# Block attention with a top-1 expert layer: one written order of four rounds for TensorE, VectorE and ScalarE

## The chip, the core and the metric

The kernel runs on one core of one Trainium2 chip. TensorE multiplies matrices (PE in the profile, and PEld for its weight loads), VectorE (DVE), ScalarE (ACT) and GpSimd (POOL) do the elementwise work, SyncE (SP) issues the transfers. The metric is the device time of one execution in microseconds, smaller is better.

## The reference

```python
def _attn_ref(q, k, v) -> np.ndarray:
...
    scores = scale * np.matmul(q, k.transpose(0, 1, 3, 2))
...
    mask = block_i >= block_j
    scores = np.where(mask, scores, -1000000000.0)
    scores = scores - np.max(scores, axis=-1, keepdims=True)
    attn = np.exp(scores)
    attn = attn / (np.sum(attn, axis=-1, keepdims=True) + 1e-09)
    return np.matmul(attn, v).astype(np.float32)

def _moe_ref(x, w_gate, w_output_gate, w1, w2) -> np.ndarray:
...
    logits = x @ w_gate
    e_idx = np.argmax(logits, axis=1)
...
    for e in range(E):
        mask = e_idx == e
...
        h = np.maximum(x[mask] @ w1[e], 0.0)
        ye = h @ w2[e]
        out[mask] = gate_w[mask, None] * eom[mask, e, None] * ye
    return out.astype(np.float32)
```

Attention over 8 batches of 8 heads, 576 positions of 64 elements each, with a mask by blocks of 64 positions, comes first; its output is the input of a layer in which each token goes to one of eight experts.

## The kernel before, in words

The work of the attention is cut into 32 pairs of heads (`Pair`, numbered p), four pairs to a batch. A pair goes through these steps, each in a round of its own, and four rounds g carry one pair further; in every round several pairs are at work, at different steps:

- `fetch` loads q and k (`nat`, six transfers on SP); `split` casts them to 16 bits on ACT (`sp0`, two pairs of buffers) and takes the remainder on POOL (`sp1`); `turn` moves both through a transposing transfer into `tr` (four buffers).
- `max_tile` 0, 1 and 2 multiply q by k into score tiles of PSUM, from which DVE takes the negated maxima of the five row tiles (`nmx`, `nmz`); `turn_max` transposes them on PE and ACT copies them out (`qe`).
- `prob_tile` 0 to 3 multiply again, with the maxima and the mask as further products, and ACT takes the exponential (`pc13`, `pc0`, `pc2`, `pcr`). Its 16-bit remainder (`lpc`, `lpcr`) is made by DVE and POOL.
- `values_odd` and `values` 0 and 1 multiply the probabilities by v (`vn`, and its 16-bit halves `vh` from ACT and `vl` from POOL) into the one tile of `ps_v`; DVE divides by the sums (`xn`), SP stores it to `x_d`, and `turn_x` transposes it on PE for the routing, copied out by ACT (`xT`).
- After the fourth pair of a batch `finish_batch` computes the routing: logits, their maxima, ranks and weights, in small operations on PE, DVE and ACT.

All score tiles, transposes and logits take the three two-bank PSUM tiles of the pool `ps_s` in rotation (`banks()`): a tile can be written when the reader of the third tile before it is done. Before the change PE's instructions stand in program order (`manual_schedule`); a list scheduler orders those of the other engines, and `high_priority` marks the maxima. The first expert's weights are loaded and split from round 120 on; from about 600 us the kernel runs the experts alone, with code that the change leaves alone.

Of the kernel before, what the change touches and what calls it, by code (L numbers as in the profile page):

```python
# [10 lines left out]
F32 = mybir.dt.float32  # L11
# [9 lines left out]
P = 128  # L21
# [5 lines left out]
def block_attention_top1_moe(  # L27
# [18 lines left out]
    R0 = 64  # L46
# [45 lines left out]
    class Pair:  # L92
# [55 lines left out]
        def max_tile(self, i):  # L148
            if i == 0:
                self.nmx = small.tile([P, NT, 2], F32, name="nmx")  # L150

            def products(os, n, c0):
                m = P * (n + 1)
                main = [o[:, c0:c0 + m].rearrange("p (n x) -> p n x", x=P) for o in os]
                for ab in range(2):
                    nc.tensor.matmul(main[ab], self.asks(0, ab, n, n + 1)[:, 0], self.keys(0, ab, 0, n + 1), start=True, stop=False)  # L156
                for ab in range(2):
                    half = slice(64 * ab, 64 * ab + 64)
                    nc.tensor.matmul(
                        main[ab][:, n, 64:P], mq[half], mk[half], start=False, stop=True  # L160
                    )
                for ab in range(2):
                    nc.tensor.matmul(
                        os[ab][:, c0 + m:c0 + m + R0], self.asks(0, ab, n, n + 1)[:, 0], self.odd(0, ab, 0, R0), start=True, stop=True
                    )

            if i < 2:
                ps = banks()
                os = [ps[:, ab] for ab in range(2)]
                if i == 0:  # L170
                    products(os, 2, 0)
                    for ab in range(2):
                        nc.tensor.matmul(os[ab][:, 448:512], self.odd(0, ab, 0, P), self.odd(0, ab, 0, R0), start=True, stop=True)  # L173
                    parts = ((2, 0, 448), (4, 448, 512))
                else:
                    products(os, 1, 0)
                    products(os, 0, 320)
                    parts = ((1, 0, 320), (0, 320, 512))
                for t, c0, c1 in parts:
                    with tc.high_priority(offset=60):  # L180
                        last_max[0] = nc.vector.tensor_reduce(self.nmx[:, t, :], ps[:, :, c0:c1], AX.X, ALU.max, negate=True)  # L181
            else:
                os = [banks().rearrange("p a n -> p (a n)") for ab in range(2)]
                products(os, 3, 0)
                self.nmz = nmzs[self.p % 2]
                for ab in range(2):
                    with tc.high_priority(offset=60):
                        last_max[0] = nc.vector.tensor_reduce(self.nmx[:, 3, ab:ab + 1], os[ab][:, 0:S], AX.X, ALU.max, negate=True)  # L188
                with tc.high_priority(offset=60):
                    nc.vector.tensor_scalar(  # L190
                        self.nmz.rearrange("p t (h c) -> p t h c", h=2)[:, :, :, 0], self.nmx, 1.0 / MS, None, ALU.mult
                    )
# [8 lines left out]
        def prob_tile(self, i):  # L201
# [4 lines left out]
            ps = banks()  # L206
# [37 lines left out]
            if i != 1:  # L244
                for ab in (slice(0, 1), slice(1, 2)) if i == 0 and self.p < NPR - 4 else (slice(0, 2),):
                    eng = nc.gpsimd if ab.stop == 1 else nc.vector
                    eng.tensor_tensor(self.pl[i][:, ab], self.pt[i][:, ab], self.high(i)[:, ab], ALU.subtract)  # L247
# [25 lines left out]
        def values(self, ab):  # L273
# [13 lines left out]
            if ab == 0:  # L287
                return
# [7 lines left out]
            )  # L296
            to = x_d[self.b * S:(self.b + 1) * S, self.hp * P:(self.hp + 1) * P]
# [697 lines left out]
    def round_of(g):  # L995

        r = g % 4
        for fn in events.get(g, ()):
            fn()
# [6 lines left out]
        if r == 0:  # L1006
            do(0, "max_tile", 0)
            do(8, "prob_tile", 3)
            do(12, "values", 1)
        elif r == 1:  # L1010
            do(1, "max_tile", 1)
            do(5, "prob_tile", 0)
        elif r == 2:
# [12 lines left out]
    with tc.manual_schedule(engines={mybir.EngineType.PE}):  # L1026
# [119 lines left out]
```

## Time and profile before

| | |
|---|---|
| median of 3 runs | 981.88 us (981.39 to 984.54) |
| the profiled execution | 982.18 us |
| its span, first to last instruction | 980.2 us |
| PE busy | 820.9 us (84%) |
| DVE busy | 567.9 us (58%) |
| ACT busy | 456.7 us (47%) |
| POOL busy | 349.9 us (36%) |
| granted TensorE clock, mean | 0.857 |

The shares are means over the whole span, in which the attention (to about 570 us) and the experts (from about 600 us) behave differently. The granted clock is a share of 2.4 GHz; at any one time it is at 1.00 or at 0.50 (1.2 GHz), and values between are means over time. In the profile L181 and L188 are the maxima, L117 the casts of q and k, L243 the exponentials, L156 the score products, L213 the products of the probability tiles, L284 the first product of the values, L306 the output transposes, L197 and L199 the transposed maxima and their copy.

### The profile page before, as it was taken

How to read it: one execution, taken by the hardware profiler on the slowest of the kernel's cores; microseconds unless marked ns; L12 is line 12 of the kernel's file. 1: busy time of each engine (PE TensorE's matmuls, PEld its weight loads, DVE VectorE, ACT ScalarE, POOL GpSimd, SP SyncE). 2: the span in 40 equal slices, each digit the busy share in tenths (PEclk: the TensorE clock that was granted, in tenths of full speed). 3: DMA queues.
4: the chain of work that ended last, by engine and by line, in shares of the span. 5: the costliest groups of instructions: out<-in, count | busy, mean ns of one | idle time of the engine just before them, and what ended most of it. 6: DMA issues, size and time to landing. Idle time of an engine off the chain costs nothing. (4 is left out here: it accounts for less than half of the span.)

```text
span 980.2 us, 22497 instructions
## 1 busy us (share of the span) xinstructions
PE 820.9 (84%) x8893; PEld 586.8 (60%) x8912; DVE 567.9 (58%) x922; ACT 456.7 (47%) x700; POOL 349.9 (36%) x389
## 2 busy tenths in 40 slices
PE   2787868777878868778786899899999999999995
PEld 1464646555556646555564686667766777677762
DVE  7835544544544544656556335778685868686560
ACT  2644433324333333344334421767675767585650
POOL 5644344234243243342505534633223234241101
PEclk9986876776776777879687789999999999999998
DMA  6766684464454474545336205697999997972331
GB/s 158 153 146 143 134 132 87 93 94 97 102 115 85 96 113 97 104 93 97 51 74 187 66 26 195 172 311 210 294 325 327 298 303 231 299 220 66 131 108 35
DMA packets 277154, 148.72 MB, mean 152 GB/s; under 512 B 230864, under 2 KB 249328, under 8 KB 277040
## 3 DMA queue, kind: packets, MB, share of 16 engines
q1 hardware_dynamic: 268992, 127.90, 52.4%
q0 software_dynamic: 8048, 19.29, 6.2%
q8 instruction: 72, 1.18, 0.5%
q14 instruction: 42, 0.34, 0.1%
HBM read 126.03 MB, written 19.34 MB: 148 GB/s over the span
## 5 line engine op out<-in xcount | busy, mean ns | idle before, releaser
L872 PEld LDWEIGHTS <-w1b 128*128 128x128 f16 (+1 forms) x2208 | 177.1, 98 | 26.2 <-issue 4.8
L872 PE MATMUL ps_s<-xt,w1b 128*128 128x256 f16 (+5 forms) x1920 | 175.1, 253 | 0.4 <-DVE w1b L751 0.3
L901 PE MATMUL ps_o<-w2b,hh 128*128 128x512 f16 (+1 forms) x541 | 162.9, 380 | 0.8 <-ACT hh L880 0.5
L751 DVE TENSOR_TENSOR w2b<-w2f,w2b 128x1024 bf16<-128x1024 f32 x80 | 92.7, 1220 | 90.1 <-ACT w2b L749 83.7
L181 DVE TENSOR_REDUCE nmx<-ps_s 128x2 f32<-128x896 f32 (+3 forms) x128 | 82.1, 683 | 82.6 <-PE ps_s L173 76.1
L156 PE MATMUL ps_s<-tr 64*128 64x384 f16 (+3 forms) x256 | 53.1, 346 | 78.7 <-ACT pc L243 47.5
L284 PE MATMUL ps_v<-vn,pc 128*128 128x65 f32 x512 | 116.8, 348 | 0.0
L146 POOL TENSOR_TENSOR vl<-vn,vh 128x448 f16<-128x448 f32 x32 | 33.2, 1037 | 226.0 <-ACT vh L145 174.8
L118 POOL TENSOR_TENSOR sp<-nat,sp 128x256 f16<-128x256 f32 (+1 forms) x126 | 100.2, 815 | 30.2 <-ACT sp L117 26.2
L247 DVE TENSOR_TENSOR lpc<-pc 128x512 f16<-128x512 f32 (+1 forms) x64 | 53.5, 836 | 98.9 <-ACT pc L243 98.8
L901 PE MATMUL ps_o<-w2b,hl 128*128 128x512 f16 x280 | 106.4, 380 | 1.2 <-DVE hl L881 0.2
L910 POOL DMA_INDIRECT out_dram<-ys,ids x38 | 50.0, 1317 | 155.2 <-ACT ys L909 91.0
L213 PE MATMUL ps_s<-tr,tr 64*128 64x384 f16 (+5 forms) x768 | 98.5, 340 | 0.0
L284 PEld LDWEIGHTS ps_v<-vn,pc 128*128 128x128 f32 x512 | 94.9, 246 | 4.3
L243 ACT ACTIVATE pc<-ps_s 128x1024 f32<-128x1024 f32 (+1 forms) x96 | 83.5, 878 | 24.7 <-PE ps_s L213 14.9
L751 DVE TENSOR_TENSOR w1b<-w1f,w1b 128x1024 bf16<-128x1024 f32 x80 | 93.0, 1219 | 1.8 <-ACT w1b L749 1.5
L213 PEld LDWEIGHTS <-tr 64*128 64x128 f16 (+1 forms) x1152 | 53.1, 110 | 67.6 <-issue 40.1
L901 PEld LDWEIGHTS <-hh 128*128 128x128 f16 x560 | 54.4, 98 | 62.6 <-issue 0.8
L117 ACT CAST sp<-nat 128x256 f16<-128x256 f32 (+1 forms) x124 | 47.5, 427 | 92.5 <-DMA tr<-sp 67.0
L213 PE MATMUL ps_s<-tr 64*128 64x256 f16 (+5 forms) x384 | 66.4, 341 | 26.6 <-DVE nmx L188 14.4
L749 ACT CAST w1b<-w1f 128x1024 f16<-128x1024 f32 x80 | 78.5, 1046 | 4.3 <-DMA w1f<-in_moe_w_dram 4.1
L749 ACT CAST w2b<-w2f 128x1024 f16<-128x1024 f32 x80 | 77.6, 1043 | 1.3 <-DMA w2f<-in_moe_w_dram 1.3
(210 smaller groups left out, 1573.3 us busy)
## 6 DMA issues: line engine op xcount, KB each, us to landing
w1f<-in_moe_w_dram SPq DMA_DIRECT2D x80, 512.0 KB
w2f<-in_moe_w_dram SPq DMA_DIRECT2D x80, 512.0 KB
nat<-in_k_dram SPq DMA_DIRECT2D x64, 128.0 KB
nat<-in_q_dram SPq DMA_DIRECT2D x64, 128.0 KB
vn<-in_v_dram SPq DMA_DIRECT2D x64, 128.0 KB
x_d<-xn SPq DMA_DIRECT2D x32, 256.0 KB
hh<-in_moe_w_dram SPq DMA_DIRECT2D x4, 512.0 KB
hl<-in_moe_w_dram SPq DMA_DIRECT2D x4, 512.0 KB
```

The costliest lines, as they stand in the source:

```text
L118: last_lo[0] = lo.tensor_tensor(sl[:, h], nat, sh[:, h], ALU.subtract)
L156: nc.tensor.matmul(main[ab], self.asks(0, ab, n, n + 1)[:, 0], self.keys(0, ab, 0, n + 1), start=True, stop=False)
L181: last_max[0] = nc.vector.tensor_reduce(self.nmx[:, t, :], ps[:, :, c0:c1], AX.X, ALU.max, negate=True)
L213: nc.tensor.matmul(os[ab], ks(kc, ab), qs(qc, ab), start=j == 0, stop=j == 3)
L243: last_exp[0] = nc.scalar.activation(self.pt[i], ap, AF.Exp, scale=SCALE)
L247: eng.tensor_tensor(self.pl[i][:, ab], self.pt[i][:, ab], self.high(i)[:, ab], ALU.subtract)
L284: nc.tensor.matmul(o, part(self.pt[1]), self.vn[:, ab], start=False, stop=False)
L749: nc.scalar.copy(hi, src)
L751: eng.tensor_tensor(lo[at], src[at], hi[at], ALU.subtract)
L872: nc.tensor.matmul(ph[:, f4].rearrange("p (h n) -> p h n", n=w), wv[:, cc, f, :], xv[:, cc], start=(k == 0), stop=(k == 3 * KD - 1))
L901: nc.tensor.matmul(py, hv[:, f, h], wv[:, f, :], start=(k == 0), stop=(k == 3 * KF - 1))
L910: nc.gpsimd.indirect_dma_start(out=out, out_offset=IOA(ap=ids[i][0:w, h, 0:1].bitcast(U32), axis=0), in_=ys[0:w], in_offset=None, bounds_c ...
```

## The change

PE, DVE and ACT now all run in program order, and the rounds are written anew. The maxima's transposes move from the end of a round to the start of the next, the values of both halves one round ahead; normalising and storing become steps of their own; the remainders (`lows`) are placed apart from the exponentials. The loads, casts and transposed loads of a pair, which stood at the head of a round, stand at its end, with new round numbers. The last row tile's maxima took two score tiles, one for each head of the pair, 576 columns each; now both heads' 512 main columns share one tile, and the 64 odd columns of each are written into a free corner (columns 256 to 320) of the tile of `prob_tile` 2, which uses 256 columns a bank (`max_rest`).

```diff
-            at(base - 12, lambda p=p: make(p))
-            at(base - 9, lambda p=p: pairs[p].split(0, nc.scalar.copy, nc.gpsimd))
-            at(base - 8, lambda p=p: pairs[p].split(1, nc.scalar.copy, nc.gpsimd))
-        at(base - 7, lambda p=p: pairs[p].turn(0))
-        at(base - 6, lambda p=p: pairs[p].turn(1))
+            at(base - 14, lambda p=p: make(p))
+            at(base - 11 if p > 3 else 2 * p - 3, lambda p=p: pairs[p].split(0, nc.scalar.copy, nc.gpsimd))
+            at(base - 10 if p > 3 else 2 * p - 2, lambda p=p: pairs[p].split(1, nc.scalar.copy, nc.gpsimd))
+        at(base - 7 if p > 3 or p == 1 else 2 * p - 1, lambda p=p: pairs[p].turn(0))
+        at(base - 6 if p > 3 or p == 1 else 2 * p, lambda p=p: pairs[p].turn(1))
     for p in range(NPR):
-        at(4 * p + 5, lambda p=p: pairs[p].fetch_v())
-        at(4 * p + 8, lambda p=p: pairs[p].split_v())
+        at(4 * p + 4, lambda p=p: pairs[p].fetch_v())
+        at(4 * p + 7, lambda p=p: pairs[p].split_v())
+        at(4 * p + 13, lambda p=p: pairs[p].store())
...
         if r == 0:
+            do(4, "turn_max")
+            do(12, "norm")
             do(0, "max_tile", 0)
             do(8, "prob_tile", 3)
-            do(12, "values", 1)
         elif r == 1:
             do(1, "max_tile", 1)
             do(5, "prob_tile", 0)
+            do(9, "lows", 3)
...
         elif r == 2:
             do(6, "prob_tile", 1)
+            do(6, "lows", 0)
             do(2, "max_tile", 2)
-            do(14, "turn_x")
+            do(10, "values_odd")
+            do(10, "values", 0)
         else:
-            do(7, "prob_tile", 2)
-            do(11, "values_odd")
-            do(11, "values", 0)
-            do(3, "turn_max")
+            ps = banks() if g < 4 * NPR + 4 else None
+            do(7, "prob_tile", 2, ps)
+            do(3, "max_rest", ps)
+            do(7, "lows", 2)
+            do(11, "values", 1)
+            if g < 4 * NPR + 11:
+                do(15, "turn_x")
+        for fn in events.get(g, ()):
+            fn()
         pay_later()
 
-    NG = 4 * NPR + 11
+    NG = 4 * NPR + 10
...
-    with tc.manual_schedule(engines={mybir.EngineType.PE}):
+    with tc.manual_schedule(engines={AT.PE, AT.Activation, AT.DVE}):
...
+        def max_rest(self, ps):
+            self.odds([ps[:, ab] for ab in range(2)], 3, 256)
+            self.nmz = nmzs[self.p % 2]
+            nmr = small.tile([P, 2], F32, name="nmr")
+            last_max[0] = nc.vector.tensor_reduce(nmr, ps[:, :, 256:320], AX.X, ALU.max, negate=True)
+            nc.vector.tensor_tensor(self.nmx[:, 3, :], self.nmx[:, 3, :], nmr, ALU.min)
+            nc.vector.tensor_scalar(
+                self.nmz.rearrange("p t (h c) -> p t h c", h=2)[:, :, :, 0], self.nmx, 1.0 / MS, None, ALU.mult
+            )
```

Three places show what moves. The first is ACT around the first exponential of pair 15; before the change it reads so (`pcr` is the fourth exponential of pair 14, `sp` the casts of q and k of pair 20, `vh` that of v of pair 15, `pc` the first two exponentials of pair 15):

```order
L243 ACTIVATE pcr<-ps_s 128x576 [waits PE_49,Activation_49]
L117 CAST sp_4095<-nat 128x5x64 [waits DMAHW7_49,DMAHW6_49,Pool_49]
L117 CAST sp_4095<-nat 128x5x64 [waits DMAHW5_49]
L117 CAST sp_4095<-nat 128x4x64
L145 CAST vh_101<-vn_99 128x7x64 [waits DMAHW6_49,DMAHW0_49,PE_49]
L243 ACTIVATE pc_3941<-ps_s 128x1024 [waits PE_49]
L117 CAST sp_4095<-nat 128x4x64
L243 ACTIVATE pc_3942<-ps_s 128x1024 [waits PE_49,Activation_49]
```

With the change, the same casts of pair 20 (here `sp_4071`) stand behind the exponentials of pair 16:

```order
L248 ACTIVATE pcr<-ps_s 128x576 [waits PE_49,Activation_49]
L248 ACTIVATE pc_4193<-ps_s 128x1024 [waits PE_49,Pool_49]
L117 CAST sp_4071<-nat 128x5x64 [waits DMAHW2_49,DMAHW7_49,DMAHW1_49,Pool_49]
L117 CAST sp_4071<-nat 128x5x64 [waits DMAHW4_49]
L248 ACTIVATE pc_4194<-ps_s 128x1024 [waits PE_49]
L117 CAST sp_4071<-nat 128x4x64
L117 CAST sp_4071<-nat 128x4x64 [waits DMAHW0_49]
L248 ACTIVATE pc_4195<-ps_s 128x512 [waits PE_49,Activation_49]
```

They have moved a pair later against the exponentials, and the exponentials no longer stand behind them within a round. The second place is PE around the last row tile's maxima; before, where the second of the two score tiles (the fourth row below) waits for ACT:

```order
L156 LDWEIGHTS tr_2656 [waits DVE_49]
L156 MATMUL ps_s<-tr_2656 128x512 [waits PE_49]
L156 LDWEIGHTS tr_2656
L156 MATMUL ps_s<-tr_2656 128x512 [waits Activation_49]
L159 LDWEIGHTS mq
L159 MATMUL ps_s<-mk,mq 128x64
```

and with the change, at the end of the third probability tile, where the odd columns (L185) are multiplied and the values of the second half (L290) follow:

```order
L218 LDWEIGHTS kext
L218 MATMUL ps_s<-qe,kext 128x256
L185 LDWEIGHTS tr_2976
L185 MATMUL ps_s<-tr_2976 128x64 [waits Activation_49]
L185 LDWEIGHTS tr_2976
L185 MATMUL ps_s<-tr_2976 128x64
L290 MATMUL ps_v<-vn_98,pc_3194 128x65 [waits DMAHW3_49]
```

The wait for ACT at the second score tile is gone with that tile, and the first odd product waits for ACT in its stead. The third place is DVE during the routing of a batch; before, its small operations lie between the maxima (`nmx`) and the remainders (`lpc`):

```order
L527 TENSOR_TENSOR z<-L,oh 128x40
L525 TENSOR_SCALAR se<-se 128x5
L529 TENSOR_REDUCE zs<-z 128x5
L188 TENSOR_REDUCE nmx<-ps_s 128x1 x2
L531 SCALAR_TENSOR_TENSOR zs<-zs,se 128x5
L190 TENSOR_SCALAR nmz_97<-nmx 128x10
L532 RECIPROCAL idg<-zs 128x5
L247 TENSOR_TENSOR lpc_3678<-pc_3675 128x512
L511 TENSOR_TENSOR rk<-ps_s,oh 128x40
L513 TENSOR_REDUCE rank<-rk 128x5
L516 SCALAR_TENSOR_TENSOR sl<-er,rank 128x5
L181 TENSOR_REDUCE nmx<-ps_s 128x2 x2
```

and with the change they stand in one piece ahead of the second score tile's maxima:

```order
L519 TENSOR_TENSOR rk<-ps_s,oh 128x40
L521 TENSOR_REDUCE rank<-rk 128x5
L524 SCALAR_TENSOR_TENSOR sl<-er,rank 128x5
L526 TENSOR_SCALAR sli<-sl 128x5
L529 TENSOR_TENSOR d<-L,mx 128x40
L532 TENSOR_REDUCE se<-d 128x5
L533 TENSOR_SCALAR se<-se 128x5
L535 TENSOR_TENSOR z<-L,oh 128x40
L537 TENSOR_REDUCE zs<-z 128x5
L539 SCALAR_TENSOR_TENSOR zs<-zs,se 128x5
L540 RECIPROCAL idg<-zs 128x5
L172 TENSOR_REDUCE nmx<-ps_s 128x2 x2
```

Between `d` and `se`, and between the two `zs`, ACT takes an exponential, so DVE goes to ACT and back twice within this piece.

## Rows read from the trace of the kernel before

**Rows 1.** windows: us, then PE, PEld, DVE, ACT, POOL busy (instructions); clock, DMA share, GB/s.
```profile
41.09:543.44 502.35, 388.15 (x4982) 283.34 (x4980) 263.64 (x522) 193.06 (x363) 190.88 (x213) 0.75 0.53 108
...
24.00:46.00 22.00, 18.70 (x294) 12.27 (x291) 17.94 (x28) 14.35 (x26) 14.06 (x17) 1.00 0.78 153
```

**Rows 2.** waits, 50 to 545 us: us in total, times, longest us.
```profile
ACT sp L117 <- DMA tr<-sp: 67.0, 21, 4.9
...
PE ps_s L156 <- ACT pc L243: 47.5, 26, 3.9
```

**Rows 3.** timeline, one pair: start, us, engine, line, operation, idle before it.
```profile
236.79 1.12 ACT L117 CAST sp<-nat 128x320 f16<-128x320 f32 x3 [2.89 <-DMA tr<-sp]
...
238.29 1.01 ACT L243 ACTIVATE pc<-ps_s 128x1024 f32<-128x1024 f32 x1
...
239.35 0.46 PE L156 MATMUL ps_s<-tr 64*128 64x512 f16 x1 [1.57 <-ACT pc L243]
```

**Rows 4.** windows, the stretch behind that wait.
```profile
239.70:249.40 9.70, 9.05 (x95) 6.47 (x95) 3.56 (x5) 2.85 (x6) 4.05 (x5) 0.50 0.30 67
```

**Rows 5.** timeline of ACT: the copy of the row maxima in three pairs.
```profile
230.99 0.69 ACT L199 COPY qe<-ps_s 128x640 f16<-128x640 f16 x1 [3.81 <-PE ps_s L197]
...
247.31 0.69 ACT L199 COPY qe<-ps_s 128x640 f16<-128x640 f16 x1 [3.80 <-PE ps_s L197]
...
267.15 0.69 ACT L199 COPY qe<-ps_s 128x640 f16<-128x640 f16 x1 [3.75 <-PE ps_s L197]
```

**Rows 6.** timeline of PE: first rows of blocks at clock 1.00.
```profile
30.66 0.45 PE L197 MATMUL ps_s<-ident,nmz 128*128 128x128 f16 x5 [0.48 <-DVE nmz L190]
...
32.85 0.34 PE L213 MATMUL ps_s<-tr 64*128 64x384 f16 x2
...
33.74 0.38 PE L213 MATMUL ps_s<-tr 64*128 64x512 f16 x2
...
36.32 0.29 PE L213 MATMUL ps_s<-tr 64*128 64x256 f16 x2 [0.19 <-ACT pc L243]
...
37.32 0.66 PE L284 MATMUL ps_v<-vn,pc 128*128 128x65 f32 x4
...
41.03 0.66 PE L284 MATMUL ps_v<-vn,pc 128*128 128x65 f32 x4
...
42.66 0.28 PE L156 MATMUL ps_s<-tr 64*128 64x256 f16 x2
...
64.20 0.77 PE L306 MATMUL ps_s<-ident,xn 128*128 128x128 f32 x5 [0.28 <-ACT pc L243]
```

**Rows 7.** timeline of PE: the same values block at clock 0.50, and what follows.
```profile
209.24 1.11 PE L284 MATMUL ps_v<-vn,pc 128*128 128x65 f32 x4
...
212.12 0.72 PE L197 MATMUL ps_s<-ident,nmz 128*128 128x128 f16 x5
```

**Rows 8.** timeline: the third probability tile and the exponential behind it.
```profile
29.89 0.29 PE L213 MATMUL ps_s<-qe,kext 64*128 64x256 f16 x2
...
30.21 0.60 ACT L243 ACTIVATE pc<-ps_s 128x512 f32<-128x512 f32 x1 [0.41 <-PE ps_s L213]
```

**Rows 9.** DVE groups by shape in those 29 pairs: xcount, busy us, mean ns.
```profile
L188 DVE TENSOR_REDUCE nmx<-ps_s 128x1 f32<-128x576 f32 x58 | 41.0, 747 | 0.0
...
L181 DVE TENSOR_REDUCE nmx<-ps_s 128x2 f32<-128x896 f32 x29 | 31.6, 1091 | 74.7 <-PE ps_s L173 74.7
```

**Rows 10.** timeline: routing work of a batch on PE and on DVE.
```profile
101.30 1.18 PE L468 MATMUL ps_s<-xT,wg 128*32 128x512 f32 x16
...
579.07 0.20 DVE L521 TENSOR_TENSOR d<-L,mx 128x40 f32<-128x40 f32 x1
...
581.14 0.19 DVE L532 RECIPROCAL idg<-zs 128x5 f32<-128x5 f32 x1
```

**Rows 11.** timeline of SP: one transposed load and the one a pair later.
```profile
37.24 2.45 SPq L125 DMA_TRANSPOSE tr<-sp  x1
...
48.53 1.27 SPq L125 DMA_TRANSPOSE tr<-sp  x1
```

More of the change, by code (lines that the diff above doesn't have):

```diff
@@ L150, in max_tile @@
                 self.nmx = small.tile([P, NT, 2], F32, name="nmx")
[L152 to L165, printed above, removed]
             if i < 2:
@@ L170, in max_tile @@
                 if i == 0:
-                    products(os, 2, 0)
+                    self.mains(os, 2, 0)
+                    self.odds(os, 2, 384)
                     for ab in range(2):
@@ L175, in max_tile @@
                 else:
-                    products(os, 1, 0)
-                    products(os, 0, 320)
+                    self.mains(os, 1, 0)
+                    self.odds(os, 1, 256)
+                    self.mains(os, 0, 320)
+                    self.odds(os, 0, 448)
                     parts = ((1, 0, 320), (0, 320, 512))
-                for t, c0, c1 in parts:
-                    with tc.high_priority(offset=60):
-                        last_max[0] = nc.vector.tensor_reduce(self.nmx[:, t, :], ps[:, :, c0:c1], AX.X, ALU.max, negate=True)
-            else:
[L183 to L192, printed above, removed]
@@ new lines, in max_tile, with mains @@
+            else:
+                ps = banks()
+                self.mains([ps[:, ab] for ab in range(2)], 3, 0)
+                parts = ((3, 0, 512),)
+            for t, c0, c1 in parts:
+                last_max[0] = nc.vector.tensor_reduce(self.nmx[:, t, :], ps[:, :, c0:c1], AX.X, ALU.max, negate=True)
+        def mains(self, os, n, c0):
+            m = P * (n + 1)
+            main = [o[:, c0:c0 + m].rearrange("p (n x) -> p n x", x=P) for o in os]
+            for ab in range(2):
+                nc.tensor.matmul(main[ab], self.asks(0, ab, n, n + 1)[:, 0], self.keys(0, ab, 0, n + 1), start=True, stop=False)
+            for ab in range(2):
+                half = slice(64 * ab, 64 * ab + 64)
+                nc.tensor.matmul(main[ab][:, n, 64:P], mq[half], mk[half], start=False, stop=True)
@@ new lines, in odds @@
+        def odds(self, os, n, c0):
+            for ab in range(2):
+                nc.tensor.matmul(
+                    os[ab][:, c0:c0 + R0], self.asks(0, ab, n, n + 1)[:, 0], self.odd(0, ab, 0, R0), start=True, stop=True
+                )
[7 more added lines that the diff above has]
+                self.nmz.rearrange("p t (h c) -> p t h c", h=2)[:, :, :, 0], self.nmx, 1.0 / MS, None, ALU.mult
+            )
@@ L199, in turn_max, with prob_tile @@
             nc.scalar.copy(self.qe, pm[:, 0:640])
-        def prob_tile(self, i):
+        def prob_tile(self, i, ps=None):
             names = ("pc13", "pc0", "pc2", "pcr")
@@ L205, in prob_tile @@
                 self.pl = [None if j == 1 else sb.tile([P, 2, n], F16, name="l" + x) for j, (x, n) in enumerate(zip(names, (512, 512, 256, S // 2)))]
-            ps = banks()
+            ps = banks() if ps is None else ps
             qe = self.qe[:, 0:512].rearrange("p (n x) -> p n x", x=P)
@@ L243, in prob_tile, with lows @@
             last_exp[0] = nc.scalar.activation(self.pt[i], ap, AF.Exp, scale=SCALE)
[L244 to L247, printed above, removed]
+        def lows(self, i):
+            for ab in (slice(0, 1), slice(1, 2)) if i == 0 and self.p < NPR - 4 else (slice(0, 2),):
+                eng = nc.gpsimd if ab.stop == 1 else nc.vector
+                eng.tensor_tensor(self.pl[i][:, ab], self.pt[i][:, ab], self.high(i)[:, ab], ALU.subtract)
         def high(self, j):
@@ L286, in values, with norm @@
                         self.splits(o, part(self.high(i)), part(self.pl[i]), 2 * c + ab, slice(0, P), False, c == 3)
-            if ab == 0:
-                return
+        def norm(self):
             o = self.pv[:, :, 0:NT * (D + 1)].rearrange("p h (t c) -> p h t c", c=D + 1)
@@ L296, in values, with store @@
             )
+        def store(self):
             to = x_d[self.b * S:(self.b + 1) * S, self.hp * P:(self.hp + 1) * P]
@@ L997, in round_of @@
         r = g % 4
-        for fn in events.get(g, ()):
-            fn()
         def do(back, name, *args):
@@ L1012, in round_of @@
             do(5, "prob_tile", 0)
+            do(9, "lows", 3)
+            if g == 4 * NPR + 9:
+                do(13, "turn_x")
         elif r == 2:
             do(6, "prob_tile", 1)
+            do(6, "lows", 0)
             do(2, "max_tile", 2)
-            do(14, "turn_x")
-        else:
-            do(7, "prob_tile", 2)
-            do(11, "values_odd")
-            do(11, "values", 0)
-            do(3, "turn_max")
+            do(10, "values_odd")
+            do(10, "values", 0)
+        else:
+            ps = banks() if g < 4 * NPR + 4 else None
[7 more added lines that the diff above has]
+            fn()
         pay_later()
-    NG = 4 * NPR + 11
+    NG = 4 * NPR + 10
     FIRST = (NG - 4, NG - 3)
-    with tc.manual_schedule(engines={mybir.EngineType.PE}):
+    AT = mybir.EngineType
+    with tc.manual_schedule(engines={AT.PE, AT.Activation, AT.DVE}):
         for g in range(NG):
```

## The prediction

> **What bounds the kernel now.** I read the windows first. From the row-maxima copy of the third pair (41.09 us) to that of the last (543.44 us) lie 29 pairs in 502.35 us, 17.32 us a pair, with PE busy 388.15 us, or 13.4 a pair, at a granted clock of 0.75 [rows 1]. The other engines are further from full: DVE 263.64 us (9.1 a pair), ACT 193.06 (6.7), POOL 190.88 (6.6), DMA share 0.53. The earlier stretch from 24 to 46 us shows the same code otherwise: clock 1.00 throughout, though PE is idle for 3.30 of its 22 us [rows 1]. So two things are lost in a pair: some 3.9 us of PE idleness, and the clock behind it.
>
> The waits say whose idleness it is. ACT sat 67.0 us, 21 times, in front of the q/k casts until a transposed load out of their buffer had landed; PE sat 47.5 us, 26 times, in front of a score product until an exponential had freed its tile [rows 2]. The timeline of one pair joins the two: ACT's cast at 236.79 had waited 2.89 us; the exponential of the first probability tile comes behind it, at 238.29; PE's second tile for the last row tile's maxima, which needs that tile's banks, starts at 239.35 after 1.57 us [rows 3]. In the 9.70 us behind the wait PE is busy 9.05 us, at clock 0.50, which is 1.2 GHz [rows 4]. Such a stretch stands behind the gap in nearly every pair. So PE's slow clock is the price of ACT's early casts, and the pair is bound by this loop rather than by any engine's work.
>
> **The change, part by part.**
>
> *The casts.* Before, ACT casts pair 20 ahead of the first exponential of pair 15; now behind the first and second exponentials of pair 16 (the order of ACT above). The buffer they write was last read by pair 18's transposed load. That load is issued after PE's fourth probability tile of pair 14, so the cast met it about one round after its issue; it now meets it about one pair later. I take this wait as gone. It can return only if SP is late, which is costed below.
>
> *PE's own work at full clock.* Adding up starts [rows 6]: 30.66 to 33.74 holds the transposed maxima, two score tiles, the fourth and the first probability tile, 3.08 us; the second has as many columns as the first (32.85 to 33.74), 0.89; third probability tile and odd values, 36.32 to 37.32, 1.00; the values of one half 41.03 to 42.66, 1.63, twice; the output transposes 0.77; the last score tile 0.3, an estimate by the two inside the 3.08. Sum 9.30 us a pair. No product is added or dropped.
>
> *The spare corner.* The last row tile's odd columns are now written beside the third probability tile, and the printed order makes this product wait for ACT. PE's last product of that tile starts at 29.89 and would be followed at about 30.00; the exponential starts at 30.21 and takes 0.60 [rows 8]. So PE waits until about 30.85: 0.85 us in each pair, behind which the values of the second half are queued. DVE's reduction waits for it too, but PE has values and output transposes (2.4 us) before it needs the result.
>
> *DVE.* One reduction over 1024 columns (1.091 x 1024/896 = 1.25), a small one (some 0.3) and a minimum (0.2) replace two of 0.747 [rows 9]: +0.25 us, so 9.4 a pair, below PE. Its fixed order puts normalising ahead of the first score tile's maxima, whose banks the first probability tile needs. I put this wait at 0.3 us: nothing below, and 1.6 above, half of the 3.30 us that PE idled between 24 and 46 us, where its 18.70 busy us are two pairs' work.
>
> *SP.* It issues the same sixteen transfers a pair. Between 37.24 and 48.53 us [rows 11] it issued just these without a gap above 0.1 us: 11.3 us, or 10.2 with the first at the 1.27 of the later row. PE's side gives 9.30 + 0.85 + 0.3 = 10.45; I take 10.6, with 10.2 and 11.3 as bounds.
>
> *The batches.* Every fourth pair brings routing work. In the kernel before such a pair takes 19.84 us against 16.32 (247.31 to 267.15, and 230.99 to 247.31) [rows 5]. Its PE part (1.18 us of logit products [rows 10], plus transposes) I put at 1.7. Its DVE part was spread between other work; now it stands between the maxima of two score tiles: d to reciprocal 2.26 us (579.07 to 581.33 [rows 10]) with two trips to ACT, and six more operations of some 0.2: 3.4 us. The maxima of the second score tile are late by that, and PE, with two probability tiles (1.78 us) to cover, then stalls on the last score tile for up to 3 us in all. Together 5.2 us a batch; bounds 4 (DVE half covered) and 7 (twice the 3.52 of now).
>
> *The clock.* A gap of 1.57 us with idleness around it was enough for the drop at 239.70 [rows 3, 4], so I expect one per batch. The values block takes 2.88 us at clock 0.50 (209.24 to 212.12 [rows 7]) against 1.63, so a stretch like that of rows 4 loses 9.05 x (1 - 1.63/2.88) = 3.9 us.
>
> *Sum over the 29 pairs*, with seven batches in them: 29 x 10.6 = 307.4, batches 7 x 5.2 = 36.4, clock 7 x 3.9 = 27.3, together 371 us against 502.35: 131 us less. The profiled execution took 982.18 us, within 0.3 of the median of 981.88; 982 - 131 = **851 us**. Start, tail and expert stage are taken as they are.
>
> **Rivals.**
>
> *The clock stays up through the batches.* It speaks for it that rows 1 show 1.00 with 15% idle; against it, that one stall is longer than the one of rows 3. Then 344 us: **824 us**. With 10.2 a pair and 4 a batch, 804.
>
> *SP becomes the bound.* Each transposed load waits for PE, and everything queues behind it. With 11.3 us a pair, the batches (36.4/29 = 1.25), and a clock drop of 3.9 us in one pair of three, the pair is 11.3 + 1.25 + 1.3 = 13.85: **881 us**. For it, SP's full stretch; against it, that q/k loads are now fetched two rounds earlier, so lateness has far to go before ACT feels it.
>
> *The clock stays low and the kernel is slower.* The 0.85 us wait in every pair and three score tiles in rotation keep PE stopping and starting. All blocks at 2.88/1.63 are 16.4 us; with 0.85, 0.3 and the batches' PE work (some 0.75) 18.3 a pair, 1.0 above now: **1011 us**. It decides once about 85% of the pairs run so, since 17.32 lies that far from 11.85 (warm, with batches) towards 18.3. Against it, rows 1: gaps of this size between 24 and 46 us left the clock at 1.00. The Trainium skill ("TensorE: Matmul & The Clock Gate", the section on PSUM-queue depth-cycling) speaks for this rival: it says that a kernel cycling through PSUM banks lets PE micro-idle between groups so often that its clock oscillates. This trace agrees for the long gaps and disagrees for short ones.
>
> *The waits only move.* With ACT's order rigid, a late load of q or k stops the exponentials as before, a time near **982**. Against it, the three rounds that the plan leaves between fetch and cast.
>
> **How the numbers follow.** The forecast has 0.42, the clock kept up 0.25, SP the bound 0.2, slower 0.08, waits moved 0.05. The range of 8 in 10 runs from 800 (below the 804 of the best case) to 905 (SP the bound, with some pairs cold besides). A measurement tells about 0.3%, 3 us, from nothing. Faster takes the first three and a part of the last, 0.9; same 0.03; slower 0.07.
>
> **What would show it.** Right: no ACT wait on a transposed load in front of a cast; 29 pairs in 330 to 405 us; a granted clock of 0.85 or more there; PE waiting some 0.85 us a pair for the third exponential at the odd product; the longest PE waits in every fourth pair, behind DVE. Wrong: a clock of 0.6 with no gap above 1 us, ACT waiting for q or k loads (SP), or an engine with a share near 0.95 that I hold to be free.

## The result and the profile after

The changed kernel takes 852.36 us (median of 4 runs, 849.81 to 854.52) against 982.75 us (median of 4, 981.39 to 984.54) for the kernel before: a ratio of 0.867, with a 95% interval of 0.864 to 0.871. The profiled execution took 849.81 us, its span is 848.2 us. Here and below a time is the median of all runs of a kernel, and a ratio compares its fast runs alone with those of the kernel before that were measured beside it.

The first view to take up again is that of the windows, from the copy of the row maxima of the third pair to that of the last, then three single pairs, then the two pieces around one stall. The columns are those of rows 1.

```profile
47.55:413.81 366.26, 312.28 (x5020) 244.73 (x5019) 259.47 (x549) 188.07 (x360) 181.96 (x206) 0.93 0.76 147
...
280.17:290.53 10.36, 9.45 (x170) 7.55 (x168) 7.43 (x15) 6.25 (x13) 5.34 (x6) 1.00 0.76 149
290.53:302.56 12.03, 11.14 (x191) 8.39 (x189) 10.13 (x22) 6.90 (x15) 5.28 (x6) 1.00 0.80 175
302.56:318.05 15.49, 12.75 (x176) 10.30 (x174) 9.35 (x28) 6.59 (x16) 9.95 (x11) 0.78 0.82 125
...
256.00:258.70 2.70, 0.94 (x12) 0.33 (x6) 2.39 (x7) 2.51 (x5) 1.30 (x2) 1.00 0.38 87
258.70:264.00 5.30, 4.86 (x62) 4.21 (x63) 1.68 (x2) 1.16 (x4) 4.83 (x6) 0.52 0.56 105
```

The 29 pairs take 366.26 us where they took 502.35 [rows 1], at a granted clock of 0.93 instead of 0.75. That is 136.1 us less; the third pair ends 6.5 us later than before (47.55 against 41.09), and what follows the last copy takes 434.4 us where it took 436.8. Together 132 us, the whole change in the profiled executions. An ordinary pair takes 10.36 us at clock 1.00, with PE busy for 9.45. The first of the two pairs that carry a batch's routing takes 12.03; the second takes 15.49 here, at a mean clock of 0.78.

The waits from 47.55 to 413.81 us say what was lost and found (total us, times, longest us):

```profile
ACT vh L145 <- DMA vn<-in_v_dram: 7.5, 3, 3.0
...
ACT sp L117 <- DMA tr<-sp: 4.0, 3, 2.8
...
PE ps_s L185 <- ACT pc L248: 23.7, 29, 2.8
PE ps_v L264 <- DVE lpcr L253: 11.9, 8, 6.7
```

The casts' wait for a transposed load has gone from 67.0 us [rows 2] to 4.0, and PE's long waits for an exponential [rows 2] have shrunk to a shorter one in each pair, 0.8 us on average, at the odd columns of the last row tile (L185).

Two stretches of the timeline show the rest. The first shows DVE, ACT and PE (one engine after the other) around the batch stall of the last two window rows, the second DVE and POOL in the last pair, which takes 24.0 us (389.81 to 413.81):

```profile
253.74 0.22 DVE L516 TENSOR_REDUCE add<-oh 128x8 f32<-128x40 f16 x1
...
256.63 0.19 DVE L540 RECIPROCAL idg<-zs 128x5 f32<-128x5 f32 x1
256.74 1.25 DVE L172 TENSOR_REDUCE nmx<-ps_s 128x2 f32<-128x640 f32 x2
257.90 0.75 DVE L253 TENSOR_TENSOR lpcr<-pcr 128x576 f16<-128x576 f32 x1
...
256.19 0.21 ACT L538 ACTIVATE zs<-zs 128x5 f32<-128x5 f32 x1 [0.80 <-DVE zs L537]
256.30 1.01 ACT L248 ACTIVATE pc<-ps_s 128x1024 f32<-128x1024 f32 x1
...
257.36 0.39 PE L178 MATMUL ps_s<-tr 64*128 64x512 f16 x2 [0.88 <-ACT pc L248]
258.70 0.20 PE L264 MATMUL ps_v<-vh,lpcr 64*128 64x65 f16 x1 [0.89 <-DVE lpcr L253]
```

```profile
393.43 8.23 DVE L253 TENSOR_TENSOR lpcr<-pcr 128x576 f16<-128x576 f32 x1
...
393.12 1.05 POOL L146 TENSOR_TENSOR vl<-vn,vh 128x448 f16<-128x448 f32 x1
394.12 2.54 POOL L759 TENSOR_TENSOR w1b<-hh,w1b 128x256 bf16<-128x256 f32 x4
396.63 2.53 POOL L759 TENSOR_TENSOR w1b<-hl,w1b 128x256 bf16<-128x256 f32 x4
399.13 3.05 POOL L759 TENSOR_TENSOR w1b<-hh,w1b 128x256 bf16<-128x256 f32 x4
```

In the batch, DVE's routing chain (253.74 to 256.82) and its two small exponentials on ACT hold up the first probability tile's exponential (256.30) and the remainder `lpcr` (257.90). PE waits for each, 0.88 and 0.89 us, and then the granted clock falls, to a mean of 0.52 in the next 5.30 us. In the last pair the remainder that takes 0.75 us everywhere else takes 8.23 us beside POOL operations that follow each other without a gap, twelve of them splits of the first expert's weights.

### The profile page after: what moved, and what is told of

The parts are those of the page before. It is cut to its first block, busy times and chain, and to the rows that moved or that the text cites. A ratio compares the mean times of both kernels' runs of the same rounds, so it can differ in the third digit from the quotient of the medians.

```text
span 848.2 us, 22555 instructions
## 1 busy us (share of the span) xinstructions
PE 743.0 (88%) x8893; PEld 547.2 (65%) x8912; DVE 563.2 (66%) x954; ACT 452.1 (53%) x700; POOL 342.7 (40%) x389
## 5 line engine op out<-in xcount | busy, mean ns | idle before, releaser
L172 DVE TENSOR_REDUCE nmx<-ps_s 128x2 f32<-128x896 f32 (+4 forms) x160 | 120.8, 790 | 29.6 <-PE ps_s L185 24.0
L918 POOL DMA_INDIRECT out_dram<-ys,ids x38 | 47.4, 1246 | 162.2 <-ACT ys L917 86.7
L290 PE MATMUL ps_v<-vn,pc 128*128 128x65 f32 x512 | 100.8, 311 | 0.0
L118 POOL TENSOR_TENSOR sp<-nat,sp 128x256 f16<-128x256 f32 (+1 forms) x126 | 91.7, 757 | 12.9 <-ACT sp L117 12.9
L218 PE MATMUL ps_s<-tr,tr 64*128 64x384 f16 (+5 forms) x768 | 89.6, 309 | 0.0
L917 ACT ACTIVATE ys<-ps_o,ids 128x512 f32<-128x512 f32 (+1 forms) x38 | 26.1, 686 | 111.8 <-PE ps_o L909 89.3
L290 PEld LDWEIGHTS ps_v<-vn,pc 128*128 128x128 f32 x512 | 81.0, 212 | 3.5 <-issue 0.4
L218 PE MATMUL ps_s<-tr 64*128 64x256 f16 (+5 forms) x384 | 62.1, 313 | 6.1 <-ACT xT L317 3.4
L316 ACT COPY xT<-ps_s 128x512 f32<-128x512 f32 x32 | 18.8, 586 | 90.0 <-PE ps_s L314 90.0
L729 POOL DMA_INDIRECT xg<-x_d,ids x38 | 47.8, 1257 | 42.8 <-DMA ids<-tab_d 13.1
```

The costliest lines, as they stand in the source:

```text
L118: last_lo[0] = lo.tensor_tensor(sl[:, h], nat, sh[:, h], ALU.subtract)
L218: nc.tensor.matmul(os[ab], ks(kc, ab), qs(qc, ab), start=j == 0, stop=j == 3)
L290: nc.tensor.matmul(o, part(self.pt[1]), self.vn[:, ab], start=False, stop=False)
L729: nc.gpsimd.indirect_dma_start(out=xg[i % NXG][0:width[i], h], out_offset=None, in_=x_d[0:nx, :], in_offset=IOA(ap=ids[i][0:width[i], h, 0 ...
L918: nc.gpsimd.indirect_dma_start(out=out, out_offset=IOA(ap=ids[i][0:w, h, 0:1].bitcast(U32), axis=0), in_=ys[0:w], in_offset=None, bounds_c ...
```

## The experiments

**1. The casts alone, in the kernel before.** ACT's casts of q and k are held behind the exponential emitted last.

```diff
-                hi(sh[:, h], nat)
+                with tc.issue_after(last_exp[0].ins) if last_exp[0] else nullcontext():
+                    hi(sh[:, h], nat)
```

> The kernel before with one edit: ACT's casts of q and k may not stand ahead of the exponential that was emitted last before them; PE's, DVE's and the rest of ACT's order, the rounds and the score tiles are as before. Theory (the early casts make the gap, the gap makes the low clock): ACT's waits for a transposed load (67.0 us, 21 times) are nearly gone, granted clock over the 29 pairs 0.90 or more, the pair 11 to 12.5 us with its share of the batches, time about 860 (840 to 890). Rival 1 (the order written for PE and DVE is needed as well, since score tiles come free late in the old order): PE still waits a microsecond or more for an exponential in most pairs, clock about 0.8, time 910 to 950. Rival 2 (the waits only move): 970 to 990.

Measured: 962.78 us, ratio 0.972 (0.960 to 0.984). Waits of this run from 41 to 520 us, ACT's first, then SP's queue:

```profile
ACT vh L146 <- DMA vn<-in_v_dram: 75.9, 23, 7.4
...
SPq L105 <- POOL sp L119: 67.4, 19, 6.4
```

The wait for transposed loads is gone from ACT's list, and in its place ACT waits 75.9 us for v in front of v's cast. In the kernel before, from 41.09 to 543.44 us, that wait was much smaller:

```profile
ACT vh L145 <- DMA vn<-in_v_dram: 20.7, 13, 3.6
```

This cast also stands ahead of the exponentials. The clock is 0.79 over the pairs. Rival 2 was right in kind, though not in its time: the wait moved. The first theory, that these casts are the cause, falls in the form in which I held it.

**2. PE kept busy in the gap, in the kernel before.** Fifty products, which nobody reads, are added to PE's work in each pair from the fifth on.

```diff
+                if self.p > 3:
+                    idle = pairs[self.p - 3].pv[:, 1, 330:458]
+                    for j in range(50):
+                        nc.tensor.matmul(idle, ident16, ident16, start=True, stop=True)
                 products(os, 3, 0)
```

> The kernel before with fifty products of 128 columns that nobody reads, put into PE's order just ahead of the last row tile's maxima, where PE idles 2 to 4 us in nearly every pair; ACT's early casts and their waits stay. Theory (the low clock is the price of the gap, and it is worth 3.9 us a pair): with PE busy in the gap the granted clock over the 29 pairs goes from 0.75 to 0.9 or more, ACT still waits for transposed loads before its casts, and the pair goes from 17.3 to some 13.5 us: time 870 to 900. Rival 1 (the loop of casts, transposed loads and exponentials sets the 17.3 us itself, the clock only follows): no change, 975 to 990. Rival 2 (the clock falls for another reason than that gap): the products come on top, some 3 to 5 us a pair, 1070 or more.

Measured: 984.94 us, ratio 1.002 (0.995 to 1.009); the profiled execution took 987.15 us. Its windows; the exponential, the filler and the work behind it in one pair; and two of its waits, from 50 to 545 us:

```profile
41.12:543.79 502.67, 421.35 (x6378) 330.33 (x6377) 265.37 (x520) 191.59 (x364) 191.27 (x213) 0.87 0.53 108
```

```profile
243.16 1.01 ACT L247 ACTIVATE pc<-ps_s 128x1024 f32<-128x1024 f32 x1
...
242.33 2.96 PE L187 MATMUL ps_v<-ident 128*128 128x128 f16 x50
245.23 0.39 PE L156 MATMUL ps_s<-tr 64*128 64x512 f16 x2
```

```profile
ACT sp L117 <- DMA tr<-sp: 109.0, 22, 8.0
...
PE ps_s L156 <- ACT pc L247: 22.5, 12, 4.5
```

The clock over the 29 pairs rose from 0.75 to 0.87, and they took 502.67 us where they had taken 502.35. ACT waited longer for its transposed loads, 109.0 us instead of 67.0. In the pair shown the exponential that frees the tile ends at 244.17, so the filler itself cost about 1 us there. In 12 of the 28 pairs PE still waits for that exponential behind the filler (the last row). In the others the filler ends at most 1.1 us after it and holds up besides the first tile's 0.4 us of products: at most some 24 us in all. PE's other work meanwhile fell by 54 us, from 388.15 to 334.30 (421.35 without the 87.05 of the filler), and the time did not follow. Rival 1 holds for this step of the clock: the 17.3 us of a pair were set by a ring of transfers, casts and exponentials, and what PE gained in its work did not shorten them. What a clock of 1.00 throughout would have given was not measured.

**3 to 5. Which written order counts.** The changed kernel with PE alone, PE and ACT, or PE and DVE in the written order; the scheduler orders the rest.

```diff
-    with tc.manual_schedule(engines={AT.PE, AT.Activation, AT.DVE}):
+    with tc.manual_schedule(engines={AT.PE}):
```

```diff
+    with tc.manual_schedule(engines={AT.PE, AT.Activation}):
```

```diff
+    with tc.manual_schedule(engines={AT.PE, AT.DVE}):
```

> The changed kernel with PE alone in its written order; ACT and DVE are ordered by the list scheduler again, out of the new rounds. Theory: since loads and casts now stand at the end of a round and are fetched two rounds earlier, the scheduler no longer puts casts in front of an exponential that must wait for a transposed load; the time stays within 15 us of the changed kernel, 840 to 870, clock over 0.9. Rival (the written order of ACT and DVE is what removes the wait): ACT waits for transposed loads again, 920 to 980.

> The changed kernel with PE and ACT in their written order and DVE given back to the list scheduler. With PE alone written it took 954 us, with all three 852, so ACT's and DVE's orders are worth 100 us between them. Theory (ACT's order is what counts: it keeps the casts from standing in front of the exponentials, and POOL and SP follow it): 850 to 870. Rival (DVE's order counts, it puts the maxima and remainders where PE needs them): 910 or more.

> The changed kernel with PE and DVE in their written order and ACT given back to the list scheduler, the counterpart of the run with PE and ACT. Theory (ACT's order counts): the casts move ahead of the exponentials again, ACT waits for transposed loads, SP's loads of q and k wait for POOL's remainders, 930 to 960. Rival (DVE's order counts): 880 or less.

Measured: PE alone 954.09 us, ratio 0.971 (0.962 to 0.979); PE and ACT 844.73 us, ratio 0.857 (0.848 to 0.865); PE and DVE 945.36 us, ratio 0.959 (0.951 to 0.968). ACT's waits with PE and DVE written, from 41 to 520 us:

```profile
ACT vh L145 <- DMA vn<-in_v_dram: 46.3, 21, 5.1
...
ACT sp L117 <- DMA tr<-sp: 24.5, 17, 3.4
...
ACT sp L117 <- DMA nat<-in_q_dram: 11.9, 4, 5.1
```

With PE and ACT written, from 41 to 420 us, its waits for loads come to 3.6 us in all (2.6 for v, 0.7 for a transposed load, 0.3 put down to a store). Without ACT's written order the time is 945 to 954 us, whatever DVE does; with it 845 to 852. So in the new rounds ACT's order is worth about 100 us, DVE's nothing that can be told (0.857 with the scheduler's, 0.867 with the written one, and the intervals overlap). For PE alone my expectation failed: the scheduler still put casts early, of q and k and of v, and both kinds wait, 39.7 us (20 times) for transposed loads and 35.7 us (16 times) for v.

**6. The casts early again, in the changed kernel.** For pairs above 3 the loads stand four rounds earlier and the casts three and four, right behind the transposed load out of their buffer, which is allotted with the casts instead of with the loads.

```diff
-            at(base - 14, lambda p=p: make(p))
-            at(base - 11 if p > 3 else 2 * p - 3, lambda p=p: pairs[p].split(0, nc.scalar.copy, nc.gpsimd))
-            at(base - 10 if p > 3 else 2 * p - 2, lambda p=p: pairs[p].split(1, nc.scalar.copy, nc.gpsimd))
+            at(base - (18 if p > 3 else 14), lambda p=p: make(p))
+            at(base - 14 if p > 3 else 2 * p - 3, lambda p=p: pairs[p].split(0, nc.scalar.copy, nc.gpsimd))
+            at(base - 14 if p > 3 else 2 * p - 2, lambda p=p: pairs[p].split(1, nc.scalar.copy, nc.gpsimd))
...
```

> The changed kernel with one thing undone: for pairs above 3 the casts of q and k stand right behind the transposed load out of the same buffer, two pairs back, as before the change (loads four rounds earlier, so that they are there). All three written orders stay. Theory: each cast waits 2 to 4 us for that transposed load with the third exponential queued behind it, PE waits for its tile, granted clock falls to 0.8 or below in most pairs, 930 to 990. Rival (the written order of PE with the spare corner is what gained, the casts matter little): PE's order gives the exponential slack, 850 to 880.

Measured: 917.06 us, ratio 0.932 (0.925 to 0.939), between theory and rival. From 52.92 to 471.88 us ACT waits in front of these casts, for transposed loads and, as the profile puts it, for a store on the same queue:

```profile
ACT sp L123 <- DMA x_d<-xn: 31.2, 9, 8.1
ACT sp L123 <- DMA tr<-sp: 28.0, 10, 5.2
```

Half of the gain is lost by the place of these casts, with the loads moved ahead of them. So they do matter, 65 us, once nothing else on ACT waits for a load; in the first experiment something else did.

**7. The kernel before with the order fixed and nothing else changed.** Rounds, score tiles and loads are the old ones; ACT and DVE follow program order.

```diff
-    with tc.manual_schedule(engines={mybir.EngineType.PE}):
+    with tc.manual_schedule(engines={mybir.EngineType.PE, mybir.EngineType.Activation, mybir.EngineType.DVE}):
```

> The kernel before, its rounds, score tiles and loads unchanged, with ACT and DVE in program order besides PE. Theory (the gain comes from the fixed order of ACT, not from the new rounds or the spare corner): no ACT wait on a transposed load, SP does not wait for POOL's remainders, 860 to 890. Rival (without the new rounds a fixed order makes PE wait for exponentials and maxima that stand behind each other): 920 or more.

Measured: 862.24 us, ratio 0.877 (0.869 to 0.885). Its windows, third to last copy:

```profile
41.09:428.13 387.04, 322.80 (x5004) 243.51 (x5001) 271.35 (x516) 187.56 (x360) 179.45 (x209) 0.91 0.73 139
```

ACT's only wait for a load in these pairs is a small one:

```profile
ACT vh L145 <- DMA vn<-in_v_dram: 4.2, 4, 1.5
```

Of the 130 us by which the medians of the changed kernel and the one before differ, 122 are there. New rounds, spare corner and earlier loads together are worth some 8 us, which the intervals (0.869 to 0.885, 0.864 to 0.871) do not quite separate from nothing. Inside the pairs they do more: the 29 pairs take 20.8 us less in the changed kernel's profile (366.26 against 387.04, an ordinary pair 10.36 against 10.83), of which its later start (6.5) and longer end (2.3) take 8.8 back.

**8. A fourth buffer for the loads of q and k, on top of the first experiment.**

```diff
-            self.nat = ld.tile([P, 2, 2, 5, D], F32, name="nat", bufs=3)
+            self.nat = ld.tile([P, 2, 2, 5, D], F32, name="nat", bufs=4)
```

> The kernel before with the casts behind the exponentials, as in the first run, and a fourth buffer for the loads of q and k. With the casts late alone it took 963 us; SP then waited 62.9 us for POOL's remainder of q and k before it could load into that pair's buffer, with the loads of v queued behind, and ACT waited 73.2 us for v. Theory (a ring through in-order queues, ACT's cast, POOL's remainder, SP's load, ACT's cast of v; the clock only follows): the fourth buffer opens it, both waits fall below 20 us, the pair goes to 13 us or less, 880 or less. Rival (the ring closes elsewhere, through the transposed loads or POOL's order): 930 to 965.

Measured: 959.55 us, ratio 0.975 (0.967 to 0.984), the same as with three buffers. SP still waits for POOL's remainder, ACT for v:

```profile
SPq L105 <- POOL sp L119: 58.0, 16, 6.4
```

```profile
ACT vh L146 <- DMA vn<-in_v_dram: 80.3, 22, 7.3
```

The ring that I had drawn, closed by the buffer of the q and k loads, was wrong; the rival holds.

**9. The odd columns ahead of the third exponential, in the changed kernel.**

```diff
-            do(7, "prob_tile", 2, ps)
+            do(7, "prob_tile", 2, ps, rest_odds(g, ps))
...
+            if then:
+                then()
             last_exp[0] = nc.scalar.activation(self.pt[i], ap, AF.Exp, scale=SCALE)
```

> The changed kernel with the odd columns of the last row tile multiplied ahead of the exponential of the third probability tile instead of behind it, so that PE's wait for this exponential (0.74 us in 30 pairs) cannot arise; the exponential waits for some 0.3 us more PE work instead. Theory (PE's work and this wait bound the ordinary pair of 10.37 us): ordinary pairs 9.6 to 9.8 us, 32 times 0.65 less, about -20 us, 830. Rival (SP's sixteen transfers bound the pair at 10.2 us or more): ordinary pairs 10.2 to 10.3, at most -5 us, 847 to 852, and PE waits for a transposed load or ACT for q and k instead.

Measured: 858.25 us, ratio 0.876 (0.871 to 0.881): not faster than the changed kernel, rather 1% slower. From 50 to 390 us PE's wait at the odd columns is gone. With the same edit in the combined kernel (11) ordinary pairs of 9.64 us (58.24 to 67.88) and 9.38 (331.10 to 340.48) occur. But in the same stretch ACT waits for loads and PE waits for the copy of the maxima, which is queued behind on ACT:

```profile
ACT vh L145 <- DMA vn<-in_v_dram: 15.1, 5, 5.4
...
ACT sp L117 <- DMA nat<-in_q_dram: 8.7, 3, 3.1
ACT vh L145 <- DMA nat<-in_q_dram: 8.6, 6, 3.2
```

```profile
PE ps_s L178 <- ACT qe L203: 13.2, 7, 5.4
```

The rival holds in kind: PE ran ahead of the loads, and what it gained came back as waits for them. Its floor of 10.2 us a pair does not, since single pairs of 9.4 us occur.

**10. The ranks two rounds later, in the changed kernel.**

```diff
         nc.vector.tensor_tensor(
             oh, er.unsqueeze(2).broadcast_to([P, NT, E]), erev.unsqueeze(1).broadcast_to([P, NT, E]), ALU.is_equal
         )
         yield
         yield
         yield
+        yield
+        yield
         pr = bank()
```

> The changed kernel with the rank products and the fifteen small DVE operations behind them two rounds later in their batch, so that they no longer stand between the maxima of two score tiles of the first round. Theory (the chain of 2.4 to 3.1 us holds up the maxima there, PE stalls some 1.8 us in two pieces, the clock then falls in about four batches of seven): the second pair of a batch 11 to 12 us in place of 12.8 to 16.8, sum -20 to -28 us, 824 to 832. Rival (the chain holds up whatever maxima or remainder it stands in front of): the stall shows up in the later round, the pair stays at 13 to 16 us, 845 to 855.

Measured: 842.32 us, ratio 0.859 (0.854 to 0.863), 1% faster, but not where the theory had it. The second pair of a batch takes 14.4 us in each of the last five batches, 71.9 in all; in the changed kernel these five took 12.8, 12.8, 16.8, 15.5 and 15.9, together 73.8, and the five third pairs behind them took 0.8 us less in sum than now. ACT and PE in one of them, and DVE's remainder in the last pair:

```profile
264.34 0.24 ACT L532 ACTIVATE d<-d 128x40 f32<-128x40 f32 x1 [1.68 <-DVE d L531]
265.37 0.21 ACT L540 ACTIVATE zs<-zs 128x5 f32<-128x5 f32 x1 [0.80 <-DVE zs L539]
265.48 0.58 ACT L248 ACTIVATE pc<-ps_s 128x512 f32<-128x512 f32 x1
```

```profile
266.11 0.24 PE L185 MATMUL ps_s<-tr 64*128 64x64 f16 x2 [2.67 <-ACT pc L248]
...
393.74 0.87 DVE L253 TENSOR_TENSOR lpcr<-pcr 128x576 f16<-128x576 f32 x1
```

The rival holds for the batches. The chain no longer holds up maxima, but its two small exponentials hold up the third probability tile's in ACT's fixed order, and PE waits 2.67 us for that one. The gain sits in the last pair of the 29: it takes 13.0 us instead of 24.0, since the remainder there falls at another point of POOL's splits and takes 0.87 us instead of 8.23. That the edit did this was not meant, and says nothing of the ranks.

**11. The first weights' splits two rounds apart, and the three edits together.**

```diff
-        for w, fn, r0, r1 in ((w1, split_w1, 4, 1), (w2, split_w2, 3, 1)):
+        for w, fn, r0, r1 in ((w1, split_w1, 4, 2), (w2, split_w2, 3, 1)):
```

> The changed kernel with the four splits of the first expert's first weights on POOL two rounds apart in place of one. Theory (the remainder on DVE at 393.43 takes 8.23 us, eleven times its 0.75, because POOL's three splits follow each other without a gap from 394.12 on, and DVE's operation ends only as these end): one split of 2.5 us stands beside it, the operation takes at most 3.5 us, the pair of 24.0 us goes to 14 to 19, -5 to -10 us, about 845. Rival (the long operation has nothing to do with POOL's stretch): it stays over 8 us and the time stays within 2 us of 852.

> The changed kernel with the three edits together: odd columns ahead of the third exponential, ranks two rounds later, splits of the first weights two rounds apart. Theory: the gains come at different places and add up, -20 -24 -7 us, about 800 (790 to 815), 29 pairs in 315 us. Rival (SP's transfers bound the pair): the pairs without batch work stay at 10.2 us or more, only the batches and the last pair gain, 820 to 830.

Measured: the splits alone 845.69 us, ratio 0.859 (0.855 to 0.863); the three edits together 833.35 us, ratio 0.848 (0.845 to 0.852). With the splits apart, DVE and POOL in the last pair:

```profile
397.63 3.14 DVE L253 TENSOR_TENSOR lpcr<-pcr 128x576 f16<-128x576 f32 x1
...
398.24 3.06 POOL L759 TENSOR_TENSOR w1b<-hh,w1b 128x256 bf16<-128x256 f32 x4
```

The long operation shrank to 3.14 us and the pair from 24.0 to 14.2, as the theory had it. Yet in this profile (850.64 us, the slowest of its six runs) the other 28 pairs took 7.0 us more than in that of the changed kernel, though their code is the same but for the place of the splits: sums over pairs vary by that much from one profile to another. The combination, the fastest kernel of this study, is 2.2% below the changed kernel. Its 29 pairs take 348.27 us against 366.26, 18 less, of which the last pair (11.1 us in place of 24.0) gives 13 and all other pairs together 5, which the 7.0 above do not set apart from nothing. The gains did not add up to my 800, because two of the three edits gain in the same place; SP's rival gave 820 to 830 and came nearer, though not by its floor of 10.2 us a pair.

## Why the prediction was right, and where its steps failed

The predicted 851 us met the measured 852.36, and several terms came out close; the reason given for them was only partly right, and that the total met to 1.4 us was luck.

*The casts* ("I take this wait as gone"): right as to the changed kernel, 67.0 us down to 4.0. But it names one of two kinds of cast that can wait. The cast of v can wait for its load in the same way, and takes over when only the casts of q and k are late (75.9 us, experiment 1). The prediction never named it. What removes both is ACT's written order: without it 945 us, with it 845 (experiments 3 to 5).

*"PE's slow clock is the price of ACT's early casts"*: this step fails as an account of the time before, as far as it was tried: with the clock at 0.87 instead of 0.75 the pair stayed at 17.3 us (experiment 2), and the 54 us that PE's work gave back went into filler and waits. That the pair is bound by a loop and not by an engine's work stands. The sum survived because it did not subtract a clock price in the ordinary pairs; it rebuilt the pair from work at clock 1.00, and that work is what bounds the pair once nothing on ACT waits for loads.

*PE's own work* (9.30 us): 9.45 busy in an ordinary pair. *The spare corner* (0.85 us): 0.74 in each pair. *DVE* (0.3 us in front of the first probability tile): not seen in the ordinary pairs; 0.15 us behind the output copies instead. Sum 10.6 against 10.36. The odd-product wait is real, and yet taking it away gains nothing, since loads then come late (experiment 9). Whether SP's issuing or the transfers themselves are late was not separated. (The bounds put for SP are slightly off: the trace of rows 11 has fourteen issues in that stretch, not sixteen, and 11.3 with the first at 1.27 is 10.1, not 10.2.)

*The batches* (5.2 us and a clock drop of 3.9 each): the first pair of a batch costs 12.03 - 10.36 = 1.7, as costed for PE. The second costs 2.4 where the clock stays up (157.79 to 170.54, 12.75 us) and 5.1 to 6.4 where it falls, which it did in four of the six second pairs among the 29; within the pair a fall so costs 2.7 to 4.0 us, where 3.9 was put. The chain (3.08 us, costed at 3.4) cost PE two waits of 0.9, not up to 3 us on the last score tile. Moving it only moved the wait (experiment 10). That the stall brings the clock down, as the step has it, is only half borne out. The last five batches have the same two waits; behind them the clock fell in three (the pairs from 252.95, 302.56 and 350.81 us) and stayed at 1.00 in two (from 157.79 and 206.74), and the earlier fall, at about 108.7, came behind another wait, of 2.19 us (to 107.53). One of the two that stayed up:

```profile
157.79:170.54 12.75, 10.05 (x176) 7.96 (x174) 9.60 (x28) 6.60 (x16) 8.62 (x10) 1.00 0.69 131
...
162.13 0.39 PE L178 MATMUL ps_s<-tr 64*128 64x512 f16 x2 [0.80 <-ACT pc L248]
163.47 0.20 PE L264 MATMUL ps_v<-vh,lpcr 64*128 64x65 f16 x1 [0.89 <-DVE lpcr L253]
```

What decides between the two is not shown.

*Not priced*: the last pair's 24.0 us, 13.6 above an ordinary one. 29 x 10.36 = 300.4 and these 13.6 leave 52 us of the 366, or 7.5 a batch with the slower early pairs, where 9.1 was put. So the sum erred by 7 us in the ordinary pairs and by 11.5 in the batches, both too high, and by 13.6 in the last pair, too low; the later start (6.5 us) less the shorter end (2.4) made up 4.1 more. That some 18 us too high met some 18 too low is luck.

*Rivals.* Clock kept up (824): true of two of the six second pairs of a batch. Slower at a low clock (1011): did not come about; the 29 waits at the odd columns, 0.8 us on average, left the clock of ordinary pairs at 1.00. The Trainium skill ("TensorE: Matmul & The Clock Gate", the section on PSUM-queue depth-cycling) says of a kernel that cycles through PSUM banks that PE idles briefly between groups so often that its clock oscillates. These ordinary pairs do not show that, with one such wait in each 10.36 us at clock 1.00; the batches, where the same waits of 0.9 us close together left the clock up twice and were followed by a fall three times, agree in part. SP the bound (881): not here; loads came late when PE was quicker (experiment 9). Waits only move (982): not in the changed kernel, but that is what the casts alone did in the kernel before (experiment 1).

*Left open.* Which link closed the ring that made a pair 17.3 us. A fourth load buffer did not open it. SP's own waits in the kernel before, from 41.09 to 543.44 us, show POOL's remainders and also PE in that ring: loads of q and k waited for the one, transposed loads for PE's probability products.

```profile
SPq L105 <- POOL sp L118: 43.8, 16, 4.7
SPq L125 <- PE ps_s L213: 43.6, 20, 3.4
```

So a slow PE may have had a share in the 17.3 us that experiment 2, with its filler in PE's way, does not show. ACT's order alone in the old rounds was not run; experiment 7 fixed DVE's with it. The first experiment with the cast of v held back as well, which would show whether two late casts without the rest of ACT's order give the whole gain, was not tried.

## What to carry to other kernels

An engine with much idle time can set the pace by the order of its queue: what counts is whether anything in it waits for a transfer while work stands behind it that another engine needs. Look for every operation of that kind, since removing one lets the next take the wait over, and here fixing the order by program text removed nearly all of them together. A low granted clock beside a wait need not be a cost; fill the gap and see whether the time moves.

## What the runs showed of the hardware

A DVE operation with two inputs in SBUF, 0.75 us long elsewhere, took 8.23 us beside a POOL operation of 1.05 us and twelve of about 0.65 without a gap between them, and 3.14 and 0.87 us where it met the same splits at other points. The Trainium skill ("SBUF — State Buffer", the section on who interferes with whom) says that such an operation and a GpSimd operation that reads SBUF exclude each other, the one behind being blocked until the first has ended. The trace agrees that DVE is blocked. It shows besides that DVE does not get in after the first: it sat through most of them. Why it got in early in one run and late in another stays open. In the kernel before, a comparison of 40 columns a lane took 3.48 us (530.58) beside the same splits, and 0.20 us (402.33) in the changed kernel, just behind them.

In the kernel before, 87.05 us of unread products in PE's waits raised the granted clock of the 29 pairs from 0.75 to 0.87 without a change in time that could be told: a ratio of 1.002 (0.995 to 1.009).
